# Attention and MLP on one core: weight sign from the exponent step, a plain maximum for fp32 scores, one v scale for batch 0, and a new order

## Chip, core, metric

One core of a Trainium2 chip. Its engines each run a list of instructions of their own and wait for one another by semaphores: TensorE (PE in the profile; its weight loads are PEld), VectorE (DVE), ScalarE (ACT), GpSimd (POOL), and SyncE (SP), whose queue issues the DMAs. The metric is the device time of one execution in microseconds.

## The reference, cut

```
q_rot, k_rot = rotate(q), rotate(k)              # q, k, v: 4 batches x 8 heads x 576 x 64
scores = q_rot @ k_rot^T / 8
attn = exp(scores - max(scores)); attn = attn / (sum(attn) + 1e-9)
x = (attn @ v) as 2304 tokens x 512
h = x @ w_in                                     # 512 x 2048
g = s * max(h, 0)**2 + b
out = g @ w_out                                  # 2048 x 512
```

The weights come in as fp64 words; q, k and v are fp32.

## The kernel before

**Tiling.** Two heads make a pair; there are 16 pairs, four to a batch. A pair has nine score tiles of 128 x 576 (eight of one head and 128 queries, one of the 64 last queries of both). Tokens are dealt to nine units: eight of 256, one for the last 64 tokens of each batch. Pairs 0 to 3 (`FQ`) and unit 0 are done in fp32, the rest with each fp32 operand split into a high and a low fp16 part.

**What must happen first.** Each of the 32 weight blocks (16 of w_in, 16 of w_out; 512 KB each) is turned from fp64 into fp32: `w_sign` writes the sign into the upper half of each word (on POOL or DVE), `w_low` the low mantissa bits into the lower half, `w_rebias` scales the upper fp64 word as an fp32 (ACT or POOL), `w_join` shifts that left by three and ORs it in (DVE). `w_gram` (PE) and `w_max` then bound the block; when all are there, `w_scale` gives the scale with which `w_hi` and `w_lo` split them. For each pair, q and k are rotated in three steps (DVE or POOL). In pairs 0 to 3, PE transposes them (`qk_T`, L767, L770), ACT copies them out (`qk_ev`), and `s_pair` (L657) makes two score tiles at once; `x_gram`, `x_top`, `all_sum` and `scales` give each pair's scale of v. Later pairs take `sumsq` on ACT, a split, and a DMA transpose.

**A score tile.** `s_max` (DVE, L681) multiplies the tile in PSUM by -1/8 (or by a scale), writes it back and leaves the minimum; `s_exp` (ACT) makes exp(min - x) with its row sum; `p_s` and `p_r` turn the sum into a factor. For half of batch 0's tiles `p_diag` makes a diagonal of it and PE transposes with it (`p_T`, L795); the other tiles go through `p_a`, `p_b` (halves), a DMA transpose (`p_t`, tile pab to pt) and `pv_sum` (L760).

**The MLP of a unit.** `mlp_in` (L887), `mlp_r` (ACT), `g_hi`, `g_lo`, `mlp_out` (L963), `out_sum`, `store`; unit 0 has fp32 versions (L913, L930).

**What sets the order.** `plan` lists the pieces with what they read and write. `ORDER` is a table that gives the sequence of all pieces, `PICKS` the engine of each piece that has a choice, and `SLOTS` which buffer each tile takes. Every engine runs its pieces in the sequence of the table and waits where a piece ahead isn't done. Helpers record many operations under one line: L410 is `act`, L402 and L404 are `ts_`, L407 is `stt`, L592 to L596 are the rotation.

Of the kernel before, what the change touches and what calls it, by code (L numbers as in the profile page):

```python
# [7 lines left out]
F32 = mybir.dt.float32  # L8
# [9 lines left out]
REBIAS = 2.0 ** -112  # L18
FQ = (0, 1, 2, 3)
G2 = ()  # L20
GP = 4
# [17 lines left out]
    "AJADAGAFAEAHAKAMALANAOAIAPDUAADfEBECDgEDEEDhEFEGAdAeAfAgDVDWDkDTD_AhDcEHDdA3EADeDiEIA4EJDXA5DYDlESELDZDrDjA6A7EMEKJjJkEN"  # L39
    "DsDtDaDqA9D1DuJrAWAwDpJlBADvA_JsA-EXAQAyAZAYJmD2DbDwBBAXDxDyDzAaAqEQEOA8BCEYD0EZEaAxBDD3ArAzJtEbA0EVARJnEcD8EPASD6AsAtD7"  # L40
    "EeEdAjAkAuEfEgJuEWERATAUJoAiD4D5J0AlBrAmBuBtEsEvDmEhAnJ1BsJ8BRJvEiBUBSEjJ2BTJ9J-BVErJpAoApEkAVEmABBED9BxFFDnE5BvAvA1AbJq"
    "J3ElEuEnBGEoJ_AcA2E6BFJ4KFJwBwBHD-KAB0BzBIKGKNByJ5B1E2DoE7JxKHBXBYKOKPJ6EpFGBKB2BZBaKIBbKQKJKKBLK4K5LAB3BNBeJ7JyKBFJBMBk"
    "EtK6KCBOBhLBJzLCKRFIBJBPE3BgFTBQBfFUKLBmEwKMBiK7BlLDB4B6B7KWBcBWKXKeCSACBnKDKSLEBoE4LFKEKYKZB5KaB8K8KfKTFhB-KbBjBpKnCVKg"
    "CUBqKhKvKoKwK9CTKcB_BdCWKdKiETClCLKUB9KjKpKqCBKVFVEqK-CACCKrKkLJCoLKLRFQKlCmKxCnLLKsKmLMKycdCMLSCNLTCpCOKzEUKtCPLNLrCDbM"
    "bObLLGCYK_FHCsCybNLULsCELVLWCZCaF7LHLOLtbPCbbQLICzC1LaLPK0CcbRExbSCXCdbTLXLQLuFkCuCvLiLbEyEzE0CtLcE1CwE-LdcecfcgCeLechE_"
    "ciMRLvFRLwLjC0LkLfMSLlC2CFC_DADBDCbWbVLYMTCICHLZLmE8bYF6L3bXK1KuCfCGLgL4MUbZbaL5F9DDMVcjCgCibhbgK2bfDMLnLxMEDODNMFCJLoLh"
    "DGL0K3F-MWE9FAChL1C3CxbiC4MXMCGHCKCQbUbbL2bjbkckCjFSMDMGL6MHL7DPCRLpLqMdMIMLDHMqMeL_DIFKL8b2b1b0CkLyC5LzFfMAMMCqMNMJMfMr"
    "CrL9C8clM3FLb3C6M4MKMBL-bcFMcmC7FNM5C9FOM6b4cnb5FiGIcoFPMabdDEC-DJMbM7FqFWMcM8FYb6brMoDFMOFXMgM9MpMhFZMlMmMicpMsFCF5F8MQ"
    "MPMjMtMuFrNAMZMYFDFgMkNONBNPbeb7blbmDKMvMxMyNCNDb8bsbnDLNQNRNENSNFNGDQFEDRNTNUNXcqNmMwMzMnNHDSNnN0dDFaFBbqbpFjbtNIFsNJNV"
    "GJGENYFtM0NoNdNebuM1NLFcM2cBcAFlb-N1GFNMGGNfNgNhFmNpcrFuFnNiN2M_NWNKNZM-Fdb_bobvN3cCN4FoNqFpNjFvcsNrNsFeN5NNcDFyODdEb9cE"  # L50
# [35 lines left out]
PICKS = (
    "VSSGGGVSSGSSGSSGSSVSSGSSVVSGSSVSSGSGVSGGSSVVSVSGGSSGSSVSSGSSGSSVSSGSSGSSGSGGSSVSSGSGGSSGGGGGGGGSVVSSSVVSSSVVSSSVVSSSVVSS"
    "SVVSSSGVSSSVVSSSVVSSSVVSSSVVSGGVVGSVVVSSVGVGSGVVSVGVGGSSSSSVGSVGSSGSSGSSVSVGSSVSSSSSVGSGVSSGSSSSSVSSSSSGVSSSVSGVVSSGSSSS"
    "SSVSSSSSSSSSGGSSVSSSSGSSSSSSSSSSVSSSGSSSSSSSSSSSSSVVSSSGVSSSVSVSSVSVSSVVSVGVSGSSVSSSVSSSSSSSGSSSVVVVVSSGVSSSGSSSVSVGVSGG"
    "VGVSSSSSSGVSSSVSSVSSVVGVVVVVVSGVSGGVVGVVVVGVSSVSSVVGVSVVSSSSSSSSSGGSSGSSGSSGVSSVGSGSSGSGSVVSSVSGSGSVSGSGSVSGVSSGSVSVSGSG"  # L90
    "VVSGSVVVVGSGVGSVVGVGSGSGVSVVSGVGSVSVSGVVSGVVVVSVSVVGSVSGSVVVVVSVSVSGSGSVVGVGSGVVVGSGVVVGVVSVVVSVVVVGSVVGVVVGSGSGVV"
)
# [57 lines left out]
def plan():  # L150
# [32 lines left out]
    def prep(pr):  # L183
# [3 lines left out]
        for nm in "v" if F else "kqv":  # L187
            if pr < GP:
                add(PE, "x_gram", pr, nm, r=[(nm, pr)], p=[("bank", "mb", pr)])
            else:  # L190
                add(ACT, "sumsq", pr, nm, r=[(nm, pr)], p=[("mx", pr)])
# [902 lines left out]
```

## Time and profile before

| | us |
|---|---|
| median of 3 executions | 614.69 (613.73 to 614.74) |
| span of the profiled execution, first to last instruction | 611.0 |
| PE busy | 584.1 (96%) |
| DVE busy | 473.7 (78%) |
| ACT busy | 412.8 (68%) |
| POOL busy | 122.7 (20%) |

The profile gives no time of its own for the profiled execution; between its span and the median lie 3.7 us. Busy time on PE is time in which any matmul is in flight, so a short wait inside a run of matmuls doesn't show as idle.

### The profile page before, as it was taken

The page shows a single profiled execution, that of the slowest core. Times are in us where ns is not written, and L with a number is a line of the kernel's source. Part 1 is how long each engine was busy: PE and PEld are TensorE (multiplying, and loading weights), DVE is VectorE, ACT ScalarE, POOL GpSimd, SP SyncE. Part 2 cuts the span into 40 slices and gives each one's busy share as a digit, 9 for nine tenths or more (in the row PEclk, how much of TensorE's full clock was granted, in tenths as well). Part 3 has the DMA queues.
Part 4 walks back from the last instruction along what each step waited for, and adds up shares of the span by engine and source line. Part 5 has one row for each costly group of instructions (what it writes and reads, how often), then busy time and mean ns, then how long its engine had stood idle before and what let it go on. Part 6 is the DMA issues. An engine that isn't in the chain of part 4 may idle for free.

```text
span 611.0 us, 12423 instructions
## 1 busy us (share of the span) xinstructions
PE 584.1 (96%) x4658; PEld 394.5 (65%) x4658; DVE 473.7 (78%) x1037; ACT 412.8 (68%) x864; POOL 122.7 (20%) x130
## 2 busy tenths in 40 slices
PE   2699999999999999999999999999999999999997
PEld 1466777566676657665765676657675766766875
DVE  5999998989999999999978879898777536533212
ACT  3599988778989998877677858568544534623322
POOL 2122334310111211111232322210110212010100
PEclk9999999899999999999999999999999999999999
DMA  8787999599774599978686976765681120361100
GB/s 317 274 279 233 282 231 220 121 201 196 181 160 92 95 198 232 188 139 197 151 150 106 179 178 131 145 145 108 142 170 26 30 74 1 79 155 36 36 1 34
DMA packets 210012, 90.32 MB, mean 148 GB/s; under 512 B 192288, under 2 KB 196768, under 8 KB 209952
## 3 DMA queue, kind: packets, MB, share of 16 engines
q1 hardware_dynamic: 209952, 89.54, 63.9%
q8 instruction: 36, 0.59, 0.4%
q14 instruction: 24, 0.20, 0.1%
HBM read 31.97 MB, written 4.72 MB: 60 GB/s over the span
## 4 chain that ended last, share of the span: by engine, by line
PE 77%; ACT 8%; DMA 6%; DVE 5%; issue 2%; POOL 1%; SPq 1%; ACTq 0%; DVEq 0%
PE px L887 25%; PE po L963 24%; PE px L760 8%; PE s L675 7%; PE po L930 4%; PE px L913 3%; DMA pt<-pab 3%; PE s L963 2%; PE s L657 2%; DVE s L681 2%; DMA x<-in_moe_w_out_dram 2%; ACT wio L410 1%; ACT p L410 1%; ACT x L410 1%; DMA x<-in_moe_w_in_dram 1%
## 5 line engine op out<-in xcount | busy, mean ns | idle before, releaser
L887 PE MATMUL px<-xa,wio 128*128 128x256 f16 x1536 | 182.2, 273 | 0.0
L963 PE MATMUL po<-wio,g 128*128 128x512 f16 x720 | 176.2, 379 | 0.0
L887 PEld LDWEIGHTS <-wio 128*128 128x128 f16 x1536 | 148.1, 98 | 33.5 <-issue 2.6
L410 ACT ACTIVATE p<-s,nm 128x576 f32<-128x576 f32 x144 | 105.6, 735 | 60.4 <-DVE s L681 52.2
L407 DVE SCALAR_TENSOR_TENSOR pab<-p,sum,pab 128x576 f16<-128x576 f32 x136 | 115.6, 866 | 9.5 <-POOL pab L404 8.1
L963 PEld LDWEIGHTS <-g 128*128 128x128 f16 x816 | 75.5, 98 | 66.5 <-issue 2.5
L681 DVE TENSOR_SCALAR_CACHE_REDUCE s<-s,sc 128x576 f32<-128x576 f32 x108 | 87.0, 819 | 17.5 <-PE s L676 17.1
L410 ACT ACTIVATE hr<-px,xc 128x512 f32<-128x512 f32 x64 | 43.5, 680 | 79.6 <-PE px L887 77.9
L905 POOL TENSOR_TENSOR g<-hr,g 128x512 f16<-128x512 f32 x35 | 42.5, 1215 | 183.6 <-DVE g L784 75.7
L410 ACT ACTIVATE pab<-p,sum 128x576 f16<-128x576 f32 x75 | 55.8, 764 | 5.0 <-DVE sum L709 3.5
L760 PE MATMUL px<-pt,v 128*64 128x320 f16 (+2 forms) x640 | 50.2, 281 | 2.8 <-DMA pt<-pab 2.7
L404 POOL TENSOR_SCALAR pab<-p,sum 128x576 f16<-128x576 f32 x28 | 24.0, 859 | 114.4 <-DVE sum L709 69.8
L410 ACT ACTIVATE hr<-hr 128x512 f32<-128x512 f32 x68 | 42.6, 627 | 1.6
L760 PEld LDWEIGHTS <-v 128*64 128x64 f16 x640 | 33.5, 110 | 15.5 <-issue 8.9
L675 PE MATMUL s<-qkT 128*128 128x512 f16 (+1 forms) x120 | 41.6, 383 | 0.0
L675 PE MATMUL s<-kS,qkT 128*128 128x512 f16 (+1 forms) x120 | 41.5, 380 | 0.0
L675 PEld LDWEIGHTS <-qkT 128*128 128x128 f16 (+1 forms) x240 | 22.2, 100 | 26.4 <-issue 6.5
L784 DVE CAST g<-hr 128x512 f16<-128x512 f32 x23 | 10.1, 438 | 37.7 <-ACT hr L410 23.4
L913 PEld LDWEIGHTS px<-x,wio 128*128 128x128 f32 x256 | 30.6, 192 | 3.9 <-issue 2.9
L905 DVE TENSOR_TENSOR g<-hr,g 128x512 f16<-128x512 f32 x29 | 19.8, 686 | 17.1 <-ACT g L410 16.9
L913 PE MATMUL px<-x,wio 128*128 128x128 f32 x256 | 32.6, 280 | 0.2 <-DVE wmx L481 0.2
L404 POOL TENSOR_SCALAR wio<-x 128x512 bf16<-128x512 f32 (+1 forms) x25 | 22.4, 898 | 51.3 <-ACT x L410 25.2
(146 smaller groups left out, 865.0 us busy)
## 6 DMA issues: line engine op xcount, KB each, us to landing
x<-in_moe_w_in_dram SPq DMA_DIRECT2D x16, 512.0 KB, 4.2
x<-in_moe_w_out_dram SPq DMA_DIRECT2D x16, 512.0 KB, 4.7
st_v<-in_v_dram SPq DMA_DIRECT2D x16, 320.0 KB, 4.4
st_q<-in_q_dram SPq DMA_DIRECT2D x16, 288.0 KB, 3.5
st_k<-in_k_dram SPq DMA_DIRECT2D x16, 288.0 KB, 3.6
out_dram<-o SPq DMA_DIRECT2D x7, 512.0 KB, 3.1
kS<-qkT SPq DMA_DIRECT2D x24, 144.0 KB, 2.7
pt<-pab SPq DMA_TRANSPOSE x152, 3.0
```

The lines of the kernel that those rows point to most:

```text
L404: eng.tensor_scalar(out=out, in0=in0, scalar1=s1, scalar2=s2, op0=op0, op1=op1)
L407: nc.vector.scalar_tensor_tensor(out=out, in0=in0, scalar=scalar, in1=in1, op0=op0, op1=op1)
L410: nc.scalar.activation(out=out, in_=in_, func=func, **kw)
L657: nc.tensor.matmul(ps[h][:, to], d["qF"][hh, t * P:(t + 1) * P], d["kF"][hh, keys], start=True, stop=True)
L675: nc.tensor.matmul(ps[rows, MAIN:2 * MAIN], lhs, kk[:, h:8:2], start=(n == 0), stop=(n == 1))
L681: nc.vector.tensor_scalar(out=T["s"], in0=T["s"], scalar1=-1.0 / 8.0 if pr in FQ else st[pr]["es"], scalar2=None, op0=ALU.mult, op1=ALU.mi ...
L760: nc.tensor.matmul(o[64 * h:64 * h + 64, c], v_rows(pr, h, k, z), p_rows(pr, 2 * (i // 4) + h)[:, k, c], start=((z, k) == todo[0]), stop=( ...
L887: nc.tensor.matmul(ph, w16[0][:, f, wz, cc], X["xa"][:, xz, c], start=(c == 0 and n == 0), stop=(c == NC - 1 and n == 2))
L905: (nc.vector if eng == DVE else nc.gpsimd).tensor_tensor(out=g[:, 1], in0=r, in1=g[:, 0], op=ALU.subtract)
L913: nc.tensor.matmul(ph, wi[:, f + 1, c * P:(c + 1) * P], xs[0]["x"][:, c, j * P:(j + 1) * P], start=(c == 0), stop=(c == NC - 1))
L930: nc.tensor.matmul(X["po"][:, j * DM:(j + 1) * DM], gs["h", j, f - f % 4][:, f % 4 * P:(f % 4 + 1) * P], wo[:, f + 1], start=(n == 1), sto ...
L963: nc.tensor.matmul(po, g[:, gz, jj], w16[1][:, f, wz, to], start=(n == 1 and i == 0), stop=(n == NF and i == 2))
```

## The change

- `w_sign` is gone. `w_rebias` is always on ACT and is now a Prelu: a negative word comes out 2^32 times larger, so that after the shift by three that exponent bit stands where the sign belongs. `w_low` fills the whole word instead of its lower half.
- In pairs 0 to 3, `s_max` is a `tensor_reduce` with maximum and negation that doesn't write the tile back. The factor 1/8 goes into `qk_ev` of q, and the exponent takes scale 1 instead of -1.
- For v of pairs 0 to 3, the four grams go into one bank, and one `v_top`, `v_total` and `v_scales` take the place of four `x_top`, `all_sum` and `scales`. The splits of all four v come after it.
- `ORDER`, `PICKS` and `SLOTS` are new throughout.

```diff
-        add((POOL, DVE), "w_sign", which, f, r=[wk], p=[("w32", which, f)])
         add((DVE, ACT, POOL), "w_low", which, f, r=[wk], p=[("w32", which, f)])
-        add((ACT, POOL), "w_rebias", which, f, r=[wk], w=[("hi", which, f)])
+        add(ACT, "w_rebias", which, f, r=[wk], w=[("hi", which, f)])
...
     def w_low(which, f, eng):
-        o = halves(w32[which][:, f + 1])[:, :, 0]
+        o = w32[which][:, f + 1].bitcast(U32)
...
         if eng == DVE:
-            ts_(o, x, 13, ALU.logical_shift_right)
+            ts_(o, wst[which, f][:, :, 0], 29, ALU.logical_shift_right)
...
-        cast(eng, hi, hi, REBIAS)
+        act(hi, hi, AF.Prelu, scale=REBIAS, alpha=SIGN)
...
-        nc.vector.tensor_scalar(out=T["s"], in0=T["s"], scalar1=-1.0 / 8.0 if pr in FQ else st[pr]["es"], scalar2=None, op0=ALU.mult,
-                                op1=ALU.min, accum_out=T["nm"])
+        if pr in FQ:
+            nc.vector.tensor_reduce(out=T["nm"], in_=T["s"], axis=AX.X, op=ALU.max, negate=True)
+        else:
+            nc.vector.tensor_scalar(out=T["s"], in0=T["s"], scalar1=st[pr]["es"], scalar2=None, op0=ALU.mult, op1=ALU.min, accum_out=T["nm"])
...
-        act(T["p"], T["s"], AF.Exp, bias=T["nm"], scale=-1.0, accum_out=T["sum"])
+        act(T["p"], T["s"], AF.Exp, bias=T["nm"], scale=1.0 if pr in FQ else -1.0, accum_out=T["sum"])
...
-        copy(eng, f, d.pop(("T", nm))[:, 0:576])
+        cast(eng, f, d.pop(("T", nm))[:, 0:576], 1.0 / 8.0 if nm == "q" else 1.0)
...
+        if F:
+            add(PE, "v_gram", pr, r=[("v", pr)], p=[("bank", "mb", 0)])
+            if pr == HP - 1:
+                add(DVE, "v_top", r=[("bank", "mb", 0)], w=[("mx", 0)])
+                add(PE, "v_total", r=[("mx", 0)], w=[("bank", "mb", 0)])
+                add(DVE, "v_scales", steps=3, r=[("bank", "mb", 0)], w=[("sc", 0)])
...
+        if not F:
+            split_v(pr)
+        elif pr == HP - 1:
+            for x in range(HP):
+                split_v(x)
...
 ORDER = (
-    "AJADAGAFAEAHAKAMALANAOAIAPDUAADfEBECDgEDEEDhEFEGAdAeAfAgDVDWDkDTD_AhDcEHDdA3EADeDiEIA4EJDXA5DYDlESELDZDrDjA6A7EMEKJjJkEN"
...
+    "AvADAIA0AAC0CzDPDQAxAwAyAFAEAzBbDfAKAJALA2AGAMAZA1AHA3ANA4C6C7C8C3C_C4C5DCApDWC9ATBdDTDADXDgC-DBDUDDI0C1DYAbDRDVI8DII9Aq"
```

What an engine's list holds changes in number too. DVE has 895 instructions before and 857 after, ACT 686 and 663, POOL 135 and 152; PE has three matmuls and three weight loads fewer. DVE loses 11 sign steps, 12 rotation steps, 12 steps of the v scales and some 20 others, and gains 9 `w_low`. POOL loses 21 sign steps and 8 rebias steps and gains 12 rotation steps, 9 `p_a` and 8 `w_low`. ACT loses 17 `w_low` and gains 8 `w_rebias`.

First place, the DMA queue from its first instruction: before,

```order
L438 DMA x_108<-in_moe_w_in_dram 128x1024
L438 DMA x_110<-in_moe_w_in_dram 128x1024
L530 DMA st_q_130<-in_q_dram 128x576
L533 DMA tab<-in_rope_dram 128x864
L534 DMA ident<-in_eye_dram 128x128
```

and after.

```order
L447 DMA x_108<-in_moe_w_in_dram 128x1024
L447 DMA x_110<-in_moe_w_in_dram 128x1024
L447 DMA x_112<-in_moe_w_in_dram 128x1024
L447 DMA x_114<-in_moe_w_in_dram 128x1024
L533 DMA tab<-in_rope_dram 128x864
L534 DMA ident<-in_eye_dram 128x128
L530 DMA st_q_118<-in_q_dram 128x576
```

Four weight blocks now go ahead of the first q, where there were two.

Second place, DVE behind the rotation of pair 0's k (st_k_174, st_q_183 are pair 2's; st_q_234 is pair 1's; x is a weight block, mx and sc belong to the scales of v): before,

```order
L592 TENSOR_TENSOR z_193<-st_k_174,tab 128x9x2x32
L402 TENSOR_SCALAR wio<-x_181 128x512
L594 TENSOR_TENSOR st_k_174<-st_k_174,tab 128x576
L564 TENSOR_REDUCE mx<-px_159 128x1
L402 TENSOR_SCALAR wio<-x_181 128x512
L592 TENSOR_TENSOR z_205<-st_q_183,tab 128x9x2x32
L402 TENSOR_SCALAR sc<-px_159 128x1
L407 SCALAR_TENSOR_TENSOR wio<-x_181,wio 128x512
L594 TENSOR_TENSOR st_q_183<-st_q_183,tab 128x576
L596 TENSOR_TENSOR st_k_174<-st_k_174,z_193 128x576
L681 TENSOR_SCALAR s_216,nm_222<-s_216 128x576
```

and after (st_q_124 and st_k_122 are pair 2's, st_q_178 is pair 1's).

```order
L589 TENSOR_TENSOR z_182<-st_q_124,tab 128x9x2x32
L589 TENSOR_TENSOR z_194<-st_k_122,tab 128x9x2x32
L591 TENSOR_TENSOR st_q_124<-st_q_124,tab 128x576
L591 TENSOR_TENSOR st_k_122<-st_k_122,tab 128x576
L593 TENSOR_TENSOR st_q_124<-st_q_124,z_182 128x576
L593 TENSOR_TENSOR st_k_122<-st_k_122,z_194 128x576
L679 TENSOR_REDUCE nm_224<-s_212 128x1
L589 TENSOR_TENSOR z_226<-st_q_178,tab 128x9x2x32
L679 TENSOR_REDUCE nm_232<-s_211 128x1
```

Between the rotation of pair 0's k and the first maximum there is nothing left but the six rotation steps of pair 2.

Third place, POOL from its first weight block on (wio is a weight's word, dg a diagonal, x a rebias in place): before,

```order
L404 TENSOR_SCALAR wio<-x_108 128x512
L404 TENSOR_SCALAR x_108<-x_108 128x512
L404 TENSOR_SCALAR wio<-x_108 128x512
L404 TENSOR_SCALAR wio<-x_152 128x512
L404 TENSOR_SCALAR wio<-x_236 128x512
L404 TENSOR_SCALAR wio<-x_243 128x512
```

and after.

```order
L413 TENSOR_SCALAR wio<-x_108 128x512
L413 TENSOR_SCALAR wio<-x_180 128x512
L413 TENSOR_SCALAR dg_270<-ident,sum 128x128
L413 TENSOR_SCALAR wio<-x_150 128x512
L413 TENSOR_SCALAR wio<-x_268 128x512
L589 TENSOR_TENSOR z_386<-st_q_297,tab 128x9x2x32
```

The first block waits for one POOL step where it waited for two or three, and a rotation (of pair 4's q) has come to POOL.

## Rows read from the trace of the kernel before

**Rows 1.** The page: busy time by engine, and DVE's busy tenths in 40 slices

```profile
PE 584.1 (96%) x4658; PEld 394.5 (65%) x4658; DVE 473.7 (78%) x1037; ACT 412.8 (68%) x864; POOL 122.7 (20%) x130
...
DVE  5999998989999999999978879898777536533212
```

**Rows 2.** Busy time by stretch: from:to, length, each engine's us (instructions), PEclk (granted clock), DMA share, GB/s

```profile
0.00:15.00 15.00, 3.83 (x27) 2.79 (x27) 8.05 (x18) 5.26 (x7) 3.69 (x8) 1.00 0.86 320
...
30.00:45.00 15.00, 14.04 (x92) 9.51 (x91) 14.40 (x36) 14.65 (x31) 3.68 (x5) 1.00 0.88 292
...
105.00:120.00 15.00, 14.15 (x77) 7.68 (x76) 13.14 (x30) 13.11 (x29) 5.81 (x5) 0.89 0.62 139
...
180.00:195.00 15.00, 15.00 (x125) 10.21 (x123) 14.90 (x32) 14.62 (x32) 2.22 (x3) 1.00 0.44 99
```

**Rows 3.** PE's waits, whole span: who for whom, us in total, times, longest

```profile
PE px L478 <- DVE wio L407: 8.7, 2, 8.2
...
PE px L760 <- DMA pt<-pab: 2.7, 4, 1.3
```

**Rows 4.** PE in order of time: start, us, instruction, [idle before <- releaser]

```profile
17.64 2.40 PE L657 MATMUL s<-qkT 64*128 64x512 f32 x8 [0.24 <-ACT qkT L410]
...
34.31 2.40 PE L657 MATMUL s<-qkT 64*128 64x512 f32 x8 [0.75 <-ACT qkT L410]
36.64 1.96 PE L795 MATMUL po<-dg,p 128*128 128x128 f32 x8
...
58.04 1.16 PE L795 MATMUL po<-dg,p 128*128 128x128 f32 x8
59.13 0.44 PE L797 MATMUL po<-dg,p 128*64 128x128 f32 x4
```

**Rows 5.** The start on POOL, ACT and DVE, in order of time

```profile
4.09 0.77 POOL L404 TENSOR_SCALAR wio<-x 128x512 bf16<-128x512 f32 x1 [3.65 <-DMA x<-in_moe_w_in_dram]
...
5.28 0.65 ACT L410 ACTIVATE x<-x 128x512 f32<-128x512 f32 x1 [3.27 <-DMA x<-in_moe_w_in_dram]
...
9.45 0.75 DVE L592 TENSOR_TENSOR z<-st_q,tab 128x576 f32<-128x576 f32 x1
...
14.55 0.76 DVE L596 TENSOR_TENSOR st_k<-st_k,z 128x576 f32<-128x576 f32 x1
...
28.95 0.74 DVE L596 TENSOR_TENSOR st_q<-st_q,z 128x576 f32<-128x576 f32 x1
```

**Rows 6.** Groups by line and shape, whole span: busy us, mean ns of one | idle before

```profile
L681 DVE TENSOR_SCALAR_CACHE_REDUCE s<-s 128x576 f32<-128x576 f32 x36 | 26.8, 769 | 4.4 <-PE s L657 3.6 <-ACT pab L410 0.8
L407 DVE SCALAR_TENSOR_TENSOR wio<-x,wio 128x512 uint32<-128x512 uint32 x32 | 23.4, 733 | 1.7 <-POOL wio L404 0.7 <-POOL x L404 0.5 <-issue 0.3
L410 ACT ACTIVATE wio<-x 128x512 uint16<-128x512 uint16 x26 | 20.1, 777 | 3.7 <-DMA x<-in_moe_w_in_dram 3.7
L410 ACT ACTIVATE x<-x 128x512 f32<-128x512 f32 x24 | 15.9, 674 | 7.6 <-DMA x<-in_moe_w_in_dram 3.3 <-POOL wio L404 2.6 <-DMA x<-in_moe_w_out_dram 1.7
L402 DVE TENSOR_SCALAR wio<-x 128x512 uint16<-128x512 uint16 x13 | 6.7, 514 | 4.8 <-ACT x L410 4.8
L404 DVE TENSOR_SCALAR sc<-sc 128x3 int32<-128x3 int32 x24 | 6.1, 253 | 0.4
L481 DVE TENSOR_REDUCE wmx<-px 128x1 f32<-128x128 f32 x16 | 4.4, 278 | 1.1 <-PE px L478 1.1
L859 DVE TENSOR_REDUCE xm<-px 128x1 f32<-128x256 f32 x8 | 3.4, 419 | 0.8 <-PE px L852 0.8
L592 POOL TENSOR_TENSOR z<-st_k,tab 128x576 f32<-128x576 f32 x2 | 3.3, 1656 | 0.0
L410 ACT ACT_TABLE_LOAD x1 | 1.3, 1283 | 0.7 <-PEq L1071 0.7
```

**Rows 7.** POOL and DVE side by side around 108 us, in order of time

```profile
108.11 1.91 POOL L592 TENSOR_TENSOR z<-st_k,tab 128x576 f32<-128x576 f32 x1
...
108.68 1.37 DVE L404 TENSOR_SCALAR sc<-sc 128x3 int32<-128x3 int32 x1
```

More of the change, by code (lines that the diff above doesn't have):

```diff
@@ L84 @@
+    "nxnsnvny"
 )
 PICKS = (
[L87 to L90, printed above, removed]
@@ L104 @@
+    "230301000101040310011201501111000033102120021413000501030021311121010210001100021001012112011000010011430310111201531010"
+    "10113200100100110121210501000011001101120131012001011100210110001100112100102100"
 )
@@ L186, in prep @@
             add(DMA, "load_x", pr, nm, w=[(nm, pr)])
[L187 to L190, printed above, removed]
+        if F:
[5 more added lines that the diff above has]
+        else:
+            for nm in "kqv":
                 add(ACT, "sumsq", pr, nm, r=[(nm, pr)], p=[("mx", pr)])
-        if pr < GP:
-            add(DVE, "x_top", pr, r=[("bank", "mb", pr)], w=[("mx", pr)])
-        add(PE, "all_sum", pr, r=[("mx", pr)], w=[("bank", "mb", pr)])
-        add(DVE, "scales", pr, steps=3 if F else 4, r=[("bank", "mb", pr)], w=[("sc", pr)])
+            add(PE, "all_sum", pr, r=[("mx", pr)], w=[("bank", "mb", pr)])
+            add(DVE, "scales", pr, steps=4, r=[("bank", "mb", pr)], w=[("sc", pr)])
         for nm in "kq":
@@ L207, in prep, with split_v @@
             add(DMA, "swap_k", pr, r=[("qkT", pr)], w=[("kS", pr)])
-        add((ACT, DVE, POOL), "v_hi", pr, r=[("v", pr), ("sc", pr)], p=[("v16", pr)])
+        if not F:
[3 more added lines that the diff above has]
+                split_v(x)
+    def split_v(pr):
+        sc = ("sc", 0 if pr in FQ else pr)
+        add((ACT, DVE, POOL), "v_hi", pr, r=[("v", pr), sc], p=[("v16", pr)])
         add(DMA, "swap_v", pr, r=[("v16", pr)], w=[("vS", pr)])
-        add(DVE, "v_lo", pr, r=[("v", pr), ("sc", pr)], w=[("v16", pr)])
+        add(DVE, "v_lo", pr, r=[("v", pr), sc], w=[("v16", pr)])
     def attend(pr, i):
@@ L439, in load_w @@
         wst[which, f] = t
-    def halves(x):
-        return x.bitcast(U16).rearrange("p (m z) -> p m z", z=2)
-    def w_sign(which, f, eng):
-        o = halves(w32[which][:, f + 1])[:, :, 1]
-        if eng == DVE:
-            ts_(o, wst[which, f].rearrange("p m t -> p (m t)").bitcast(U16).rearrange("p (m z) -> p m z", z=4)[:, :, 3], 0x8000, ALU.bitwise_and)
-        else:
-            ts_(o.bitcast(BF16), wst[which, f][:, :, 1].bitcast(F32), 0.0, ALU.mult, 1.0, ALU.mult, eng=nc.gpsimd)
     def w_low(which, f, eng):
-        o = halves(w32[which][:, f + 1])[:, :, 0]
+        o = w32[which][:, f + 1].bitcast(U32)
         x = wst[which, f].rearrange("p m t -> p (m t)").bitcast(U16).rearrange("p (m z) -> p m z", z=4)[:, :, 1]
         if eng == DVE:
-            ts_(o, x, 13, ALU.logical_shift_right)
+            ts_(o, wst[which, f][:, :, 0], 29, ALU.logical_shift_right)
         elif eng == ACT:
@@ L459, in w_low, with w_rebias @@
             ts_(o, x, 2.0 ** -13, ALU.mult, FLOOR, ALU.add, eng=nc.gpsimd)
-    def w_rebias(which, f, eng):
+    def w_rebias(which, f):
         hi = wst[which, f][:, :, 1].bitcast(F32)
-        cast(eng, hi, hi, REBIAS)
+        act(hi, hi, AF.Prelu, scale=REBIAS, alpha=SIGN)
     def w_join(which, f):
@@ L548, in top16 @@
         return x.bitcast(BF16).rearrange("p (e t) -> p e t", t=2)[:, :, 1]
-    def x_gram(pr, nm):
-        d = st[pr]
-        if "G" not in d:
-            d["G"] = bank()
-        i, x = "qkv".index(nm), d[nm]
-        o, n = d["G"][:, i * P:(i + 1) * P], x.shape[1]
-        for t in range(0, n, 2):
-            t = min(t, n - 2)
-            y = top16(x[:, t:t + 2].rearrange("p t d -> p (t d)"))
-            nc.tensor.matmul(o, y, y, start=(t == 0), stop=(t == n - 2))
-    def x_top(pr):
-        d, c = st[pr], cols(pr)
-        d["mx"] = small("mx", 3)
-        nc.vector.tensor_reduce(out=d["mx"][:, c], in_=d["G"][:, c.start * P:3 * P].rearrange("p (i m) -> p i m", m=P), axis=AX.X, op=ALU.max)
@@ L566, in cols, with v_gram @@
-    def cols(pr):
-        return slice(2 if pr in FQ else 0, 3)
-    def all_sum(pr):
-        c = cols(pr)
-        if pr < GP:
-            o = st[pr]["mb"] = st[pr].pop("G")[:, 3 * P:3 * P + c.stop - c.start]
-            nc.tensor.matmul(o, ones16b, top16(st[pr]["mx"][:, c]), start=True, stop=True)
-        else:
-            o = st[pr]["mb"] = bank()[:, 0:c.stop - c.start]
-            nc.tensor.matmul(o, ones16b, top16(st[pr]["mx"][:, c]), start=True, stop=True)
-    def scales(pr):
-        d, c = st[pr], cols(pr)
+    def v_gram(pr):
+        if "v" not in vs:
+            vs["v"] = bank()
+        o, x = vs["v"][:, pr * P:(pr + 1) * P], st[pr]["v"]
+        for t in range(0, 10, 2):
+            y = top16(x[:, t:t + 2].rearrange("p t d -> p (t d)"))
+            nc.tensor.matmul(o, y, y, start=(t == 0), stop=(t == 8))
@@ new lines, in v_top, with v_total, v_scales @@
+    def v_top():
+        vs["mx"] = small("vmx", HP, 1)
+        nc.vector.tensor_reduce(out=vs["mx"], in_=vs["v"].rearrange("p (i m) -> p i m", m=P), axis=AX.X, op=ALU.max)
+    def v_total():
+        nc.tensor.matmul(vs["v"][:, 0:HP], ones16b, top16(vs["mx"]), start=True, stop=True)
+    def v_scales():
+        vv = small("vsc", 2 * HP + 2, 1)
+        t = vv[:, 2:]
+        for pr in range(HP):
+            st[pr]["sc"], st[pr]["iv"] = vv[:, pr:pr + 3], vv[:, HP + pr:HP + pr + 3]
+        yield from pow2(t[:, 0:HP], vs["v"][:, 0:HP], t[:, HP:2 * HP])
@@ L580, in scales, with all_sum @@
+    def all_sum(pr):
+        o = st[pr]["mb"] = bank()[:, 0:3]
+        nc.tensor.matmul(o, ones16b, top16(st[pr]["mx"]), start=True, stop=True)
+    def scales(pr):
+        d = st[pr]
         t = small("sc", 7, 8)
         d["sc"], d["iv"], d["es"] = t[:, 0:3], t[:, 3:6], t[:, 6:7]
-        yield from pow2(d["sc"][:, c], d["mb"], d["iv"][:, c])
-        if c.start == 0:
-            stt(d["es"], d["iv"][:, 0:1], -1.0 / 8.0, d["iv"][:, 1:2], ALU.mult, ALU.mult)
+        yield from pow2(d["sc"], d["mb"], d["iv"])
+        stt(d["es"], d["iv"][:, 0:1], -1.0 / 8.0, d["iv"][:, 1:2], ALU.mult, ALU.mult)
```

113 lines of the change are left out of this document (58 added, 55 removed).

## The prediction

> **What bounds the kernel now.** First the busy times [rows 1]: PE is busy 584.1 of 611.0 us. Its idle 27 us are what can be won without taking work from PE. Then the stretches [rows 2]: 0 to 15 PE has 3.83 us, 30 to 45 it has 14.04, 105 to 120 it has 14.15 at a granted clock of 0.89, and by 180 it is full, 15.00 of 15. So the end is set by PE's work plus what it loses early. Then PE's waits [rows 3]: 8.7 us for DVE's weight words, nearly all before the first matmul, and 2.7 us in four waits for a DMA transpose, the longest 1.3.
>
> Then PE in order of time [rows 4]. Its first score pair stands at 17.64, the second at 34.31. A busy PE isn't a fast PE there: the eight diagonal matmuls at 36.64 take 1.96 us, the same eight at 58.04 take 1.16, and the pair at 34.31 takes 2.40. That is the pace of the lower of the two clock levels (1.2 against 2.4 GHz), though the records of these stretches show 1.00; before it rose, PE had worked without a wait from 34.31 on. DVE is what PE waits for until then: from 9.45 it works almost without a gap [rows 1, 5], and it is 14.40 of 15 us busy in 30 to 45 [rows 2].
>
> **The first score pair.** Its chain before: rotation of q from 9.45, of k to 14.55 + 0.76 = 15.31 [rows 5], then transpose and copy, 17.64: 2.33 us behind the rotation. After: DVE can join the first weight block when POOL's one step is done, 4.09 + 0.77 = 4.9 [rows 5]. Ahead of the rotations stand four joins at 0.73, three `w_low` and one maximum at 0.28 [rows 6]. `w_low` on DVE writes 32-bit words and has no row; it lies between the 16-bit step at 0.51 and the join at 0.73, and I take 0.55, nearer the first, as both have one input. That is 2.92 + 1.65 + 0.28 = 4.9, so 9.8. The data is there: blocks follow one another by 1.19 us (work on the first starts at 4.09, on the second at 5.28, [rows 5]), the fourth is in at 7.7, and table, identity and q have (864 + 128 + 576)/1024 of a block's bytes, 1.8 us: 9.5. Six rotation steps at 0.75 end at 14.3, the pair follows at 16.6. Lead: 1.0 us; no lead if q comes 1 us late.
>
> **The second score pair.** DVE's steps from 15.31 to the end of pair 1's rotation (28.95 + 0.74 = 29.69, [rows 5]) took 14.4 us. By the row means [rows 6] they are 12 rotation steps (9.0), two maxima (1.5), three joins (2.2), two 16-bit steps (1.0), four reduces (1.1) and seven tiny steps of the v scales at 0.253 (1.8): 16.6, so neighbours' overlap makes it 0.87 of the sum. After, there are 12 rotation steps, two maxima, two joins, one reduce and two reciprocals (taken at 0.253): 9.0 + 1.5 + 1.5 + 0.3 + 0.5 = 12.8, times 0.87 is 11.1. From 14.3 that ends at 25.4, with half a microsecond for waits at 25.9: 3.8 us sooner. The pair stood 34.31 - 29.69 = 4.6 behind that rotation: 30.5. But PE now does two diagonal transposes ahead of it, at the low pace 2 x 2.4 = 4.8 us: the pair comes at 30.5 if DVE's work covers both, at 35.3 if it covers none; I take the middle, 32.9. At full pace the two are worth 2 x (1.16 + 0.44) = 3.2 us [rows 4], less 0.3 for a weight gram that now comes later: 2.9 us of work done sooner. The lead, in PE's work at full pace, is then 34.31 - 32.9 + 2.9 = 4.3, with 1.9 and 6.7 as ends; I put **-4.0 us**, and take the first pair's 1.0 as the low end. From there on PE has work, and a lead counted in its work stays to the end.
>
> **The edits by themselves.** Of the 13 16-bit steps on DVE eleven are signs: -5.7 us; nine more `w_low`: +5.0. The maximum: a reduce takes 0.278 for 128 columns and 0.419 for 256, so 1.10 ns a column and 0.771 for 576, against 0.769 for what it replaces [rows 6]: nothing, 36 times. One scale of v: three reduces and nine tiny steps fewer, one of 4 x 128 columns (0.70): about -1.3. Twelve rotation steps go to POOL: -9.0 on DVE. So DVE loses some 11 us by these rows. That beyond the start is worth nothing while PE is full [rows 2]; if PE weren't full, it would be a gain, not a cost. The one scale makes all four splits of v wait for the fourth v; on DVE the rotation of pair 3 and the joins stand around them, and their reader, the first `pv_sum`, comes after four fp32 `mlp_in0` far behind: nothing. On ACT 17 `w_low` go (-13.2 us at 0.777) and 8 `w_rebias` come (+5.4 at 0.674) [rows 6]. A Prelu has no row; with one operand and 512 columns I take it at the 0.674 of the scaled copy, which lies nearest. 1/8 and the exponent's sign ride on steps that are there: nothing.
>
> **Later waits.** In the table's sequence, PE work that stands between a `pv_sum` and the last transpose that it reads is at most 1.1 us at six of the 32 before, three of them zero; after, the least is 1.8, the next 2.4. I take half of the 2.7 us [rows 3]: **-1.3**, ends -2.7 and 0. The 0.89 at 105 to 120 is 3.3 us at half clock, 1.65 us of work; before it fell PE had waited for scores. DVE is less late now, so I give it an even chance to go: **-0.7**, ends -1.65 and 0. A new sequence makes waits of its own: a stretch like 105 to 120 loses 0.85 idle and 1.65 by the clock, 2.5 us; I allow a third of one: **+0.8**, ends 0 and 2.5. The last matmul, its sum and its store end the kernel as before: nothing.
>
> **Sum:** -4.0 - 1.3 - 0.7 + 0.8 = -5.2. The profiled span is 611.0; the median 614.69 lies 3.7 above it, and I leave these 3.7 as they are: 605.8 + 3.7 = **609.5 us**.
>
> **Rivals.**
> - *More at the start.* The lead is 6.7 (DVE covers both transposes, or PE's pace rises sooner), the DMA waits go (2.7) and the clock holds (1.65): -11.0, 603.7. For it: PE's list puts pair 1's and 2's transposes of q, a diagonal transpose and the grams of v in a row. Against: nothing in the trace shows the pace rise before 34.
> - *The start is no sooner.* Four weight blocks go ahead of q, PE stays at the low pace, and only the first pair's 1.0 us is left: 613.7. For it: the chain goes through ACT and PSUM buffers too, where scores of one pair must be read before the next.
> - *Rotations on POOL starve PE (slower).* Three rotations are on POOL before, seven after, all of pairs 4 and later. One takes 3 x 1.66 = 5.0 us there [rows 6] against 3 x 0.75 on DVE: 2.7 us later. PE is full from 180 and DVE is 14.90 of 15 busy, so slack is short. If all four new ones are late by that, 10.9 us: 614.7 - 4.0 + 10.9 = 621.6; it decides from two of them on (5.4, 616.1). Against: PE lost nothing at the three before. In [rows 7] a DVE step on three numbers, 0.253 on average [rows 6], lasts 1.37 us while POOL rotates for 1.91: DVE stood behind it. The Trainium skill (SBUF — State Buffer, "SBUF: two separate sides") calls the port pair that both share an exclusive lock, held for the whole instruction; the trace agrees there. By that rule twelve steps could hold DVE for 12 x 1.66 = 19.9 us where it saves 9.0 itself, 10.9 net, and the time would be 620.4 with the rest of the sum unchanged.
> - *Prelu and Exp don't share a table.* Then each of 32 steps would load twice, 64 x 1.283 = 82 us on ACT [rows 6], which is 14.65 of 15 us busy at 30 to 45 [rows 2]: about 695. The changed kernel's list on ACT has one table load, as before's, which speaks against it. The Trainium skill (ScalarE: Activation LUTs, "Table sets: the hidden batching unit") has a load wherever functions of different sets follow one another; no row shows Prelu's set.
>
> **How the numbers follow.** Forecast 609.5, own range 606.5 to 612.5: 0.53. More at the start 603.7: 0.22. No sooner 613.7: 0.14. POOL 616 to 622: 0.10. Table: 0.01. A measurement of this kernel tells 0.2%, 1.2 us, from no change. Faster are the first two and a little of the third: 0.77; same 0.12; slower 0.11. The range takes in the first, half of the second and the third: 603.7 to 614.0.
>
> **What would show it.** Right: first pair near 16.6, second before 34 with two diagonal transposes ahead of it; fewer than 2 us of waits for pt; PE full from 180; `w_rebias` at 0.67. Wrong: PE idle behind rotations on POOL after 120; clock below 1 in more slices; ACT late with `w_rebias`; the maximum on DVE well over 0.77.

## The result, and the profile after

The changed kernel takes **620.68 us** (median; 618.81 to 621.88) against 614.42 of the kernel before in the same comparison: ratio **1.010, 95% interval 1.007 to 1.013**. It is slower by 6.3 us; 609.5 was forecast, and the time lies above the range. The profiled execution took 620.73 us with a span of 619.0.

First the page of the kernel after: busy times, and DVE's and POOL's tenths in 40 slices, to be held against [rows 1].

```profile
span 619.0 us, 12370 instructions
...
PE 585.1 (95%) x4655; PEld 396.9 (64%) x4655; DVE 486.0 (79%) x963; ACT 400.1 (65%) x841; POOL 162.2 (26%) x147
...
DVE  5888999999999999999999998997886654613102
...
POOL 0245313325032343332442352232111110100110
```

DVE has 74 instructions fewer and yet is busy 12.3 us longer (473.7 before). Of the 74, 36 are a second step of each `s_max` of pairs 0 to 3, the read of its minimum, which the plain maximum doesn't have (it reached some 0.06 us beyond the first step); its row before:

```profile
L681 DVE DVE_READ_ACCUMULATOR s<-s 128x1 f32 x36 | 5.0, 139 | 0.0
```

POOL went from 122.7 to 162.2. PE's work is the same (585.1 busy us for 584.1), so 7 of the 8 us of the span are time in which PE stands. The stretches tell where; kernel before, then after (columns: stretch, its length, busy us and instructions of PE, PEld, DVE, ACT, POOL, then PE's clock, the DMA share, GB/s).

```profile
0.00:120.00 120.00, 99.33 (x814) 69.68 (x815) 107.40 (x251) 95.87 (x205) 37.37 (x49) 0.99 0.87 248
120.00:440.00 320.00, 317.22 (x2553) 209.01 (x2552) 290.68 (x626) 249.20 (x533) 62.04 (x61) 1.00 0.77 157
```

```profile
0.00:120.00 120.00, 101.13 (x834) 74.17 (x835) 103.38 (x199) 86.08 (x192) 38.44 (x41) 0.96 0.86 252
120.00:440.00 320.00, 308.65 (x2461) 201.99 (x2460) 302.15 (x595) 235.40 (x503) 102.66 (x88) 1.00 0.74 154
```

Between 120 and 440 PE lacks 11.4 us where it lacked 2.8: 8.6 us, about the whole difference of the spans. There DVE does 31 instructions fewer in 11.5 us more, and POOL's 62 us have become 103. PE's four longest waits of that stretch in the kernel after (us, times, longest):

```profile
PE px L851 <- POOL g L845: 3.3, 3, 1.9
PE po L962 <- DVE o L416: 2.2, 2, 1.4
PE s L672 <- ACT p L419: 2.2, 6, 0.9
PE px L886 <- DVE xa L416: 1.0, 1, 1.0
```

Before, the only such row there was the DMA transpose's 2.7 us [rows 3]. Now PE waits for results of POOL (the adds of the norm, `x_add`), of DVE, and of ACT, which itself waits for DVE. One place shows how DVE comes to be late: POOL and DVE of the kernel after, in order of time (start, duration).

```profile
294.31 1.40 POOL L589 TENSOR_TENSOR z<-st_q,tab 128x576 f32<-128x576 f32 x1 [2.23 <-DVE st_q L593]
294.39 2.40 DVE L416 SCALAR_TENSOR_TENSOR xa<-x,xs,xa 128x1024 f16<-128x1024 f32 x1 [0.16 <-ACT xa L419]
...
295.87 2.18 POOL L591 TENSOR_TENSOR st_q<-st_q,tab 128x576 f32<-128x576 f32 x1 [0.16 <-POOL z L589]
...
296.72 1.95 DVE L416 SCALAR_TENSOR_TENSOR pab<-p,sum,pab 128x576 f16<-128x576 f32 x1
296.85 1.36 PE L886 MATMUL px<-xa,wio 128*128 128x256 f16 x11 [0.99 <-DVE xa L416]
```

The two engines take turns, each for a whole instruction. DVE's `x_lo` (the low half of a unit's scaled tokens, tile xa) starts 0.08 us behind POOL's rotation step, which ends at 295.71; it ends 1.08 us later, at 296.79 (it takes 1.28 when alone, a median of seven). POOL's next step, begun at 295.87, ends 1.26 us after that, at 298.05; and `p_b`, begun at 296.72, ends 0.62 us after that. PE waited 0.99 us for `xa`.

Over the whole trace, 41 of the 136 `p_b` (0.81 us alone) begin with over 0.25 us of a POOL step still to run; 40 of these end 0.60 to 0.62 us after that step's end, however long it was. `p_b` over 0.9 us: 14 before, 38 after. An estimate of the whole takes, for DVE's instructions beside a POOL step, the time above the lower quartile of their own form: by it POOL made DVE's work 20.6 us longer before and **46.4 us** after (another grouping of the forms moves either by about 1 us). Without that DVE would have gone from 453.1 to 439.6: the saving came, and about twice as much was taken back.

### The profile page after: what moved, and what is told of

The parts are those of the page before. It is cut to its first block, busy times and chain, and to the rows that moved or that the text cites. A ratio compares the mean times of both kernels' runs of the same rounds, so it can differ in the third digit from the quotient of the medians.

```text
span 619.0 us, 12370 instructions
## 1 busy us (share of the span) xinstructions
PE 585.1 (95%) x4655; PEld 396.9 (64%) x4655; DVE 486.0 (79%) x963; ACT 400.1 (65%) x841; POOL 162.2 (26%) x147
## 4 chain that ended last, share of the span: by engine, by line
PE 49%; DVE 32%; issue 6%; ACT 5%; DMA 4%; SPq 2%; POOL 1%; DVEq 0%; ACTq 0%; POOLq 0%
PE po L962 15%; PE px L886 14%; DVE pab L416 8%; DVE s L681 6%; PE px L759 4%; DVE wio L416 4%; PE s L672 3%; PE px L912 3%; PE s L654 2%; ACT p L419 2%; PE s L962 2%; DMA pt<-pab 2%; DVE nat L416 2%; DVE nm L679 1%; PE po L929 1%
## 5 line engine op out<-in xcount | busy, mean ns | idle before, releaser
L962 PE MATMUL po<-wio,g 128*128 128x512 f16 x720 | 170.8, 379 | 2.3 <-DVE o L416 2.2
L416 DVE SCALAR_TENSOR_TENSOR pab<-p,sum,pab 128x576 f16<-128x576 f32 x136 | 131.8, 980 | 4.2 <-POOL pab L413 2.2
L904 POOL TENSOR_TENSOR g<-hr,g 128x512 f16<-128x512 f32 x37 | 47.7, 1291 | 184.0 <-DVE g L783 105.7
L413 POOL TENSOR_SCALAR pab<-p,sum 128x576 f16<-128x576 f32 x37 | 32.7, 886 | 119.3 <-DVE sum L708 74.6
L419 ACT ACTIVATE pab<-p,sum 128x576 f16<-128x576 f32 x71 | 53.6, 768 | 10.5 <-DVE sum L708 9.8
L783 DVE CAST g<-hr 128x512 f16<-128x512 f32 x29 | 12.7, 437 | 43.0 <-ACT hr L419 32.6
L679 DVE TENSOR_REDUCE nm<-s 128x1 f32<-128x576 f32 x36 | 26.3, 748 | 4.6 <-PE s L654 3.5
```

Of the source, the lines that this page charges most:

```text
L413: eng.tensor_scalar(out=out, in0=in0, scalar1=s1, scalar2=s2, op0=op0, op1=op1)
L416: nc.vector.scalar_tensor_tensor(out=out, in0=in0, scalar=scalar, in1=in1, op0=op0, op1=op1)
L419: nc.scalar.activation(out=out, in_=in_, func=func, **kw)
L679: nc.vector.tensor_reduce(out=T["nm"], in_=T["s"], axis=AX.X, op=ALU.max, negate=True)
L783: nc.vector.tensor_copy(out, in_)
L904: (nc.vector if eng == DVE else nc.gpsimd).tensor_tensor(out=g[:, 1], in0=r, in1=g[:, 0], op=ALU.subtract)
```

## The experiments

**Theory P**: POOL's added load makes DVE's instructions longer, DVE is the engine that feeds PE from 60 to 430 us, and so PE loses time. **Rivals**: S, the new sequence on PE and DVE is worse by itself; E, one of the edits of arithmetic costs; later P2, rotations finish late on POOL. Medians in us; busy times from each kernel's profiled execution. The kernel before was run again in every comparison, with medians from 613.40 to 614.42, and the ratios are to those; so a difference between two kernels of different comparisons is uncertain by about 1 us, and by more where the executions of one kernel spread wider.

| kernel | median | ratio to before, interval | POOL | DVE | PE busy in 120:440 |
|---|---|---|---|---|---|
| before | 614.42 | | 122.7 | 473.7 | 317.2 |
| after | 620.68 | 1.010 (1.007 to 1.013) | 162.2 | 486.0 | 308.7 |
| b_more_pool | 634.25 | 1.033 (1.030 to 1.036) | 208.5 | 506.7 | 305.6 |
| a_short_pool | 606.19 | 0.987 (0.984 to 0.990) | 93.6 | 453.3 | 319.9 |
| b_short_pool | 614.03 | 1.001 (0.999 to 1.003) | 73.8 | 461.2 | 316.0 |
| a_short_rot | 613.30 | 0.999 (0.996 to 1.001) | 149.7 | 474.2 | 314.8 |
| a_rot_dve | 615.93 | 1.003 (1.001 to 1.005) | 128.9 | 481.4 | 313.1 |
| a_xadd_dve | 619.09 | 1.009 (1.006 to 1.011) | 158.2 | 486.1 | 309.9 |
| a_rot_xadd_dve | 613.38 | 1.000 (0.998 to 1.002) | 120.5 | 480.0 | 314.8 |
| a_casts_act | 630.66 | 1.027 (1.025 to 1.030) | 102.8 | 472.9 | 302.6 |
| b_sign_max | 617.02 | 1.006 (1.003 to 1.008) | 98.2 | 463.9 | 317.3 |
| b_sign24_max | 610.66 | 0.994 (0.992 to 0.996) | 108.9 | 466.0 | 318.0 |

### More work on POOL, the kernel before otherwise untouched (b_more_pool)

```
+            if x["pick"] and a[-1] == POOL and x["fn"] in ("rotate", "qk_hi", "v_hi", "p_a", "w_hi", "g_lo"):
+                nc.gpsimd.tensor_tensor(out=extra, in0=tab[:, :, 0:32], in1=tab[:, :, 32:64], op=ALU.mult)
```

> The kernel before, its sequence untouched, with one more multiply on POOL (128x288, table times table, into a tile nobody reads) behind each of POOL's 88 rotation steps, splits of q, k, v and of weights, casts of p and low halves of g. PE, DVE and ACT have the same instructions in the same order. Theory P (DVE stands behind POOL while POOL works on SBUF, and DVE's lateness becomes PE's idle time): 88 more at some 0.7 us are 60 us more on POOL, about the step from before to after (122.7 to 162.2) and a half more; DVE's busy time rises by 0.2 to 0.3 of that, 12 to 18 us, and the time by 4 to 9 us, to 618 to 623. Theory S (the new sequence on PE and DVE is worse by itself, POOL is only along): 613.5 to 616, DVE busy within 3 us of 473.7. Theory E (one of the edits costs): as S.

634.25 us, 20.6 above before's 613.64 in the same comparison: P's direction, over twice its size. POOL has 85.8 us more, DVE 33.0 us more with the very same 1037 instructions (0.38 us for each of POOL's), and the span is 20.6 longer. Nobody reads what POOL wrote there. Waits for POOL's results hardly rose: PE's come to 1.2 us (0.4 before), those of `p_b` to 9.3 (8.1 before). S and E can't make this, since nothing of the change is in it. Two groups of DVE's on the page of b_more_pool (xcount, then busy us, mean ns):

```profile
L408 DVE SCALAR_TENSOR_TENSOR pab<-p,sum,pab 128x576 f16<-128x576 f32 x136 | 130.3, 973 | 11.0 <-POOL pab L405 9.3
...
L682 DVE TENSOR_SCALAR_CACHE_REDUCE s<-s,sc 128x576 f32<-128x576 f32 x108 | 86.5, 816 | 9.9 <-PE s L677 9.9
```

`p_b`, which works on SBUF, goes from 866 to 973 ns. `s_max`, which reads and writes PSUM, stays at 816 (819 before). So it isn't DVE that got slower; it is steps of DVE's with inputs in SBUF that stand behind POOL's.

### Shorter work on POOL, the changed kernel otherwise untouched (a_short_pool)

```
+        return x if not late or x.shape[-1] in (P, DM) else x[:, 0:1] if len(x.shape) > 2 else x[:, 0:64]
...
-            ts_(out, in_, scale, ALU.mult, 1.0, ALU.mult, eng=nc.gpsimd)
+            ts_(few(out), few(in_), scale, ALU.mult, 1.0, ALU.mult, eng=nc.gpsimd)
```

and in the same way in `rotate`, `g_lo` and `x_add`; the tiles that are then part written keep their buffers.

> The changed kernel with the same instructions in the same order on every engine, but from about 113 us on POOL's rotation steps, splits of q, k and v, casts of p, adds of the norm and most low halves of g work on 64 columns or fewer (their results are left incomplete). Theory P: POOL falls from 162 to about 85 us, DVE's stretch from 46 to under 25, DVE busy to 460 to 470, PE's idle time from 60 us on from 13 to under 7, the time to 609 to 614. Theory S: PE keeps its idle time, 617 to 621, though DVE gets faster. Theory E: 617 to 621 too.

606.19 us: 14.5 less than the changed kernel, with the same lists on PE, DVE, ACT and SP. DVE fell by 32.7 to 453.3, and `p_b` to 830 ns. The stretches of a_short_pool, and one of DVE's groups on its page:

```profile
0.00:120.00 120.00, 99.45 (x835) 72.76 (x836) 103.57 (x200) 86.60 (x192) 39.00 (x41) 0.97 0.87 252
120.00:440.00 320.00, 319.91 (x2589) 211.41 (x2588) 283.96 (x621) 245.45 (x525) 48.56 (x91) 1.00 0.76 160
```

```profile
L420 DVE SCALAR_TENSOR_TENSOR pab<-p,sum,pab 128x576 f16<-128x576 f32 x136 | 111.3, 830 | 5.6 <-ACT pab L423 3.4
```

PE is full: 319.91 of 320, and no row of its waits is left in this stretch. P holds; S and E, which expected 617 to 621, fall. The place shown above reads there:

```profile
284.44 0.32 POOL L595 TENSOR_TENSOR z<-st_q,tab 128x64 f32<-128x64 f32 x1 [1.61 <-DVE st_q L599]
284.61 1.28 DVE L420 SCALAR_TENSOR_TENSOR xa<-x,xs,xa 128x1024 f16<-128x1024 f32 x1 [0.26 <-ACT xa L423]
285.82 0.81 DVE L420 SCALAR_TENSOR_TENSOR pab<-p,sum,pab 128x576 f16<-128x576 f32 x1
```

1.28 for 2.40 and 0.81 for 1.95, the same two instructions. (POOL's own results come sooner here too, so this run alone doesn't part the turns on SBUF from POOL's lateness; b_more_pool does for the kernel before, since there the waits for POOL hardly rose.)

### The same on the kernel before (b_short_pool)

The edit is that of a_short_pool, on the old sequence (without `x_add`, which isn't on POOL there).

> The counterpart of a_short_pool on the kernel before: its own sequence, and from about 113 us on its POOL's casts of p, splits of q, k and v, most low halves of g and the two later rotations work on 64 columns or fewer (their results are left incomplete). It tells what the two sequences are worth with POOL out of the way; a_short_pool took 606.2. Theory P: in the kernel before, PE is full from 180 us although POOL works, so there is little to give back: 611 to 614, and the new sequence is worth some 6 us by itself, which POOL then takes and more. The other theory (the sequences are alike, and shortening POOL is worth the same 14 us, or half of it, in both): 600 to 608.

614.03 us, no change, though DVE lost 12.5 us. In the old sequence POOL's work from about 113 us on cost nothing: DVE had 290.7 busy us in the 320 from 120 to 440, and room to be late. With most of POOL's later work out of the way the changed kernel is better by 614.03 - 606.19 = 7.8 us. So S is turned round: the new sequence together with the edits is better, and POOL takes 14.5 us from it. How much of the 7.8 is the sequence's own stays open, since the edits of the sign and the maximum alone gave 3.6 us in the old one (b_sign24_max below).

### Which work on POOL it is (a_short_rot, a_rot_dve, a_xadd_dve, a_rot_xadd_dve)

The first keeps of a_short_pool's edits the one in `rotate` alone; the other three move steps to DVE (a_rot_dve is shown; the others name `"x_add"`, or both).

```
+        if e == POOL and late:
+            x, z, cos, sin = x[:, 0:1], z[:, 0:1], cos[:, 0:1], sin[:, 0:1]
```

```
+    for kk in pick:
+        if pick[kk] == POOL and kk[0] == "rotate":
+            pick[kk] = DVE
```

> The changed kernel, every list as it is, but the twelve rotation steps that POOL does after 113 us work on 64 columns (q and k of those pairs are left part unrotated). Nothing else is shortened. Theory P1: POOL 19 us less, DVE 9 to 12 us less of its 33, and of the 14.5 us that shortening all steps gave a like share, 4 to 6 us: 614 to 617. Theory P2: nearly all of it, 606 to 611.

613.30: 7.4 us for twelve steps, half of the 14.5, and between the two expectations. POOL has 12.5 us less and DVE 11.8, nearly one for one: no other step on POOL lengthens DVE's work so much for its time (of the lengthening in the changed kernel 18.0 us fall to the 21 rotation steps, which have 35.4 us of POOL's 162.2; 13.7 to the 37 `g_lo`).

> The changed kernel in its own order with all seven of POOL's rotations (21 steps) on DVE. Theory P1 (what costs is that POOL and DVE take turns on SBUF): POOL falls by 41 us, DVE gains 21 x 0.75 = 15.8 us of its own and loses the 18 us by which POOL's rotation steps lengthened its work, so DVE stays at 482 to 490 and the time at 617 to 622. Theory P2 (what costs is that rotations end late on POOL, the rival of the prediction): the waits behind them go, 609 to 614.

615.93, 4.8 less, again in between. DVE does some 15.8 us of rotations more and is busy 4.6 us less: here a rotation step is cheaper on DVE than beside it. DVE's busy time alone doesn't give the 4.8 (in 120:440 it has 300.67, 1.5 less than the changed kernel, while PE has 4.5 more). No row of the changed kernel shows PE or ACT waiting for a rotation on POOL, so P2 has no row for it, but how the 4.8 splits between the turns and the sooner end of the rotations stays open.

> The changed kernel in its own order with the six adds of the norm (units 2 to 4) on DVE in place of POOL; PE waited 3.3 us straight for POOL there. If these waits are part of the loss: DVE 3 to 4 us more of its own, 2 us less of stretch, the three waits under 1 us, 616 to 619. If they only stand for lateness that comes from elsewhere: 619 to 622, with the waits on the same rows put down to DVE.

619.09, 1.6 less, at the bound between the two expectations. This isn't clear of noise: the intervals overlap (1.006 to 1.011 and 1.007 to 1.013), and so do the executions (618.35 to 620.85, and 618.81 to 621.88 of the changed kernel). PE's straight waits for POOL's adds (3.3) turned into 1.3 for DVE's, so the waits went, but a gain from it isn't shown.

> The changed kernel in its own order with both the seven rotations and the six adds of the norm on DVE. Rotations alone gave 4.8 us (615.9 against 620.7), adds alone 1.6 (619.1). If the two add up: 613 to 615.5, POOL at 120 to 125 us, as in the kernel before. If DVE is full and can't take both: 616 to 619.

613.38, 7.3 less than the changed kernel, clear of noise: the kernel stands where before stood, with POOL at 120.5 where before had 122.7. That the two add up (4.8 + 1.6 = 6.4) fits, but the share of the adds is as unclear here (the interval ends at 1.002, that of a_rot_dve begins at 1.001). Its stretch from 120 to 440:

```profile
120.00:440.00 320.00, 314.80 (x2525) 206.63 (x2524) 301.24 (x626) 238.00 (x511) 77.63 (x71) 1.00 0.76 155
```

DVE is busy 301.24 us here, nearly as in the changed kernel (302.15), and yet PE has 6.2 us more. It does 626 instructions in it instead of 595. So the sum of DVE's busy time isn't what decides. Which of POOL's steps delay what PE needs next, and which end late themselves, these runs don't part.

### POOL's casts given to ACT (a_casts_act)

```
+        if pick[kk] == POOL and kk[0] in ("p_a", "qk_hi", "v_hi", "w_hi"):
+            pick[kk] = ACT
```

> The changed kernel in its own order, with POOL's casts of p (37), first splits of q, k (8), of v (8) and of weights (10) given to ACT: 47 us off POOL, some 48 us on ACT, DVE's and PE's lists unchanged. Theory P: DVE's stretch falls by 8 to 12 us, time 612 to 618, unless ACT then ends last. Theory S: 618 to 622. ACT late instead: PE waits for p and x from ACT grow by over 5 us, over 622.

630.66, 10 us slower than the changed kernel, though POOL fell to 102.8 and DVE to 472.9. PE and DVE wait for ACT instead: PE's scores for exps 6.9 us in 120:440 (2.2 in the changed kernel), DVE's `p_b` for casts of p 6.3 us in nine waits. This was the third case named, ACT late. So "less on POOL" is no recipe by itself: the same work in ACT's queue stands ahead of exps that PE waits for.

### The edits without the order (b_sign_max, b_sign24_max)

b_sign_max, on the kernel before (`w_low` as in the changed kernel, `w_sign` empty, `s_max` a plain maximum with 1/8 in `qk_ev`):

```
-        cast(eng, hi, hi, REBIAS)
+        act(hi, hi, AF.Prelu, scale=REBIAS, alpha=SIGN)
```

> The kernel before with its own sequence and engines, and the two edits of arithmetic alone: no sign step, the sign with the scaling on ACT for all 32 weight blocks (8 come over from POOL), whole words from the low step, the plain maximum with 1/8 on q. The scales of v stay one a pair. Theory P: POOL loses some 25 us before 115 us, DVE 6 us: 610 to 615. Theory S: 610 to 615 too. Theory E (an edit costs): 617 to 622.

617.02, 3.4 slower than before: the lower end of E. ACT's rows between 60 and 130 us say where; the kernel before, then b_sign_max:

```profile
ACT x L410 <- DMA x<-in_moe_w_out_dram: 1.7, 1, 1.7
```

```profile
ACT x L411 <- DMA x<-in_moe_w_out_dram: 7.2, 3, 2.9
```

Eight scalings came from POOL's queue into ACT's at places where POOL used to wait for the block; now ACT waits, with exps behind it. b_sign24_max takes that away: only the 24 blocks whose scaling is on ACT anyway get the sign there.

```
+    def on_act(which, f):
+        return pick["w_rebias", (which, f)] == ACT
```

> The kernel before with its own sequence, plain maximum, and the sign with the scaling for the 24 weight blocks whose scaling is on ACT there; the other 8 keep sign and scaling on POOL. So ACT gets no step more than before. Theory A (the two edits cost 3.4 us in the old order because the 8 scalings that came to ACT stand in its queue for weight blocks: 7.2 us of waits against 1.7): 610 to 614, ACT's waits for weight blocks under 3 us. Theory B (the sign with the scaling, the whole words or the plain maximum cost by themselves): 616 to 619.

**610.66 us**, faster than both kernels (0.994, interval 0.992 to 0.996), ACT's waits for weight blocks 1.5 us in that stretch. Theory A holds: neither the plain maximum nor, on the 24 blocks that have them here, the sign with the scaling and the whole words cost anything. That the place of the eight scalings makes the 3.4 us rests on ACT's waits in these two runs.

## Why the prediction was wrong, step by step

- **The start: right in total, partly by luck.** The first pair came at 17.36 (16.6 said, 17.64 before): 0.3 us of the 1.0 that were forecast. The second came with two diagonal transposes ahead of it at 32.99 (32.9 said). Rows of PE in the kernel after, to be held against [rows 4], and the last rotation step of pair 1, to be held against the last of [rows 5]:

```profile
17.36 1.22 PE L654 MATMUL s<-qkT 64*128 64x512 f32 x2
...
26.39 2.07 PE L794 MATMUL po<-dg,p 128*128 128x128 f32 x8
...
31.56 1.14 PE L794 MATMUL po<-dg,p 128*128 128x128 f32 x8
...
32.99 1.30 PE L654 MATMUL s<-qkT 64*128 64x512 f32 x8
```

```profile
26.76 0.74 DVE L593 TENSOR_TENSOR st_k<-st_k,z 128x576 f32<-128x576 f32 x1
```

  That rotation ended at 27.50, where 25.9 was said. PE worked without a wait from 23.5 on, so what stood ahead in PE's own list set the pair's time, not DVE; that the middle between 30.5 and 35.3 came so close is luck. The pace rose already ahead of the pair, at 30.6. That the lead then stays to the end, "from there on PE has work", is what failed: it stays where PE is full behind it, as a_short_pool shows with its 7.8 us (5.2 were forecast for everything), and in the changed kernel PE isn't (308.65 of 320).
- **DMA waits: right in kind.** 2.7 became 1.8 (1.3 us was taken off).
- **The clock: missed.** It kept 1.00 at 105 to 120, as was given an even chance, but PE waited 2.84 us for an exp at 34.9 and the granted clock then was 0.5 for 10.2 us (3.4 before): at half pace 5.1 us of work against 1.7. It varied between executions of the same instructions: a_short_rot and a_xadd_dve, which do the same until 113 us, had 3.4 us of it. This is part of the 6.3 us: of the changed kernel's four executions the one with a mean clock of 0.997 took 618.81, the three with 0.989 to 0.991 took 620.63 to 621.88. By these some 2 us may be the clock's; the one at 0.997 is still 4 us above the slowest of before's four in the same comparison.
- **The edits by themselves: right.** `w_rebias` 674 ns, as said, the maximum 748 (771 said, and the read of the minimum behind it, which the sum left out, is gone too), `w_low` on DVE 417 (550 taken), one table load. No wait of PE's for the shared scale of v shows. ACT's group of `w_low` even went from 777 to 666 ns.
- **The step that failed** is "So DVE loses some 11 us by these rows. That beyond the start is worth nothing while PE is full", with "Twelve rotation steps go to POOL: -9.0 on DVE". Two things were wrong in it. DVE's work was priced by means of rows as if POOL stood still: DVE's bare work fell by some 13.5 us by the estimate above (11 forecast), but POOL's steps lengthened it by 25.8 more, so that DVE rose by 12.3. And PE's fullness from 180 was taken from the trace of before as if it were a given; it hung on the room that DVE had there. The "new waits" of +0.8 had to be 8.6, what PE lacks more from 120 to 440.
- **POOL's load was read too narrowly.** Only the four new rotations were priced. The letters of the engine table also moved to POOL nine casts of p, six adds, five first splits of v, four of q and k and two low halves (while 21 steps of the weights' conversion left it, all before 120 us). Shortening the twelve later rotation steps gives 7.4 of the 14.5 us back; the other half belongs to the rest of POOL's later work, of which the pieces that were on POOL before are part, and these runs don't divide it further.
- **The slower rival happened.** "Rotations on POOL", at 0.10, gave 616 to 622 and, by the hold of DVE behind twelve rotation steps, 620.4; 620.7 came. The Trainium skill (SBUF — State Buffer, "SBUF: two separate sides") has the port pair that DVE and GpSimd share as an exclusive lock: a GpSimd step, or a DVE step with two SBUF inputs or in a 2-port mode, holds it for its whole instruction if it starts first. The trace agrees with that step by step: 40 of the 41 `p_b` that begin well behind a POOL step end 0.60 to 0.62 us after it. The near agreement of the totals is partly luck, since the rival's sum took all of it from twelve rotation steps, and the runs give about half to the rotations. What spoke against it, "PE lost nothing at the three before", was the weak reason: b_short_pool shows that before had room on DVE for it, which the changed kernel has less of (302.15 of 320 busy, for 290.68). [Rows 7] had the mechanism in plain sight.

## What to carry to other kernels

An engine's saved instructions are worth their row means only if nothing new runs beside them on the memory that both use; when work goes from DVE to POOL, sum both engines over the stretch, and take from the trace how much longer DVE's steps on SBUF are beside POOL (here 0.4 us for each us of POOL in b_more_pool, nearly one for one beside the rotation steps). That an engine was full before says nothing of after: ask how much room its feeder has (at 291 of 320 us POOL's later work cost nothing). The busy sum alone isn't enough: with DVE at 301 to 302 of 320, PE had 308.7 in the changed kernel and 314.8 with the rotations and adds on DVE. A step moved to another queue also moves its waits there, ahead of all that stands behind it.

## What the runs showed of the hardware

- DVE and POOL take turns on SBUF for whole instructions, in both directions: `p_b` ends 0.60 to 0.62 us after the POOL step it stands behind, and POOL's rotation steps, 1.40 us at the least, lasted up to 2.40 in the changed kernel. Not every step of DVE's on SBUF is held: ten reciprocals of row sums that began there with over 0.25 us of a POOL step still to run took their usual 0.15 us. DVE's work on PSUM isn't touched where it was measured: `s_max` with a scale lasts 816 to 821 ns on average with POOL at 73.8, 122.7, 162.2 or 208.5 us.
- ACT writes whole 32-bit words faster than every second 16-bit one, in the same number of 512 elements (26 such steps in the old order, in b_sign_max, took 665 ns): kernel before, then after (mean ns behind the busy time).

```profile
L410 ACT ACTIVATE wio<-x 128x512 uint16<-128x512 uint16 x26 | 20.1, 777 | 3.7 <-DMA x<-in_moe_w_in_dram 3.7
```

```profile
L419 ACT ACTIVATE wio<-x 128x512 uint32<-128x512 uint16 x9 | 6.0, 666 | 0.1
```

- A Prelu with a scale costs what a scaled copy costs, 674 ns for 512 columns, and stands between exps with no further table load.
